# MoE steps ahead of the last score tile, shared squares, alternating PSUM banks and a reordered opening in a fused attention and mixture-of-depths kernel

## The chip, the cores and the metric

The kernel runs on one core of a Trainium2 chip. The metric is the device time of one execution in microseconds; the median of three runs of the kernel before is 230.48 us (229.37 to 230.82). The profiled execution took 229.61 us, with 227.8 us between its first and its last instruction; all times in a profile count from that first instruction.

Five engines work side by side, each through its own list of instructions in order: PE (TensorE) for matrix products and transposes, ACT (ScalarE), DVE (VectorE), Pool (GpSimd, here used nearly only to issue loads and stores) and SP (SyncE, which issues other transfers). An engine waits when its next instruction needs something that another engine or a transfer has not finished.

## The reference

Attention with squared ReLU in place of a softmax, for 8 batches of 12 heads, 448 tokens, 64 values a head; then a mixture-of-depths layer: of each batch's 448 tokens the 128 with the highest gate score go through a small two-layer network, and its gated result is added to their rows.

```python
scores = scale * np.matmul(q, k.transpose(0, 1, 3, 2))
attn = np.maximum(scores, 0.0) ** 2 / S
attn_out = np.matmul(attn, v)
x = attn_out.transpose(0, 2, 1, 3).reshape(B, S, H * D)      # (8, 448, 768)

scores = np.einsum('bsd,d->bs', x, w_gate)
out = x.copy()
for b in range(B):
    top_idx = np.argpartition(-scores[b], capacity)[:capacity]   # 128 of 448
    xe = x[b, top_idx]
    h = np.maximum(xe @ w1, 0.0)                                 # 768 -> 1024
    ye = h @ w2                                                  # 1024 -> 768
    g = 1.0 / (1.0 + np.exp(-scores[b, top_idx]))
    out[b, top_idx] = x[b, top_idx] + g[:, None] * ye
```

## The kernel before

Two heads make a pair, and a batch has six pairs (`hp` 0 to 5); there are 48 pairs (`t`). For a pair, PE transposes q and k into one PSUM bank, DVE copies them to SBUF, PE makes four score tiles (c = 0 to 3; the first three hold two heads side by side, the last one both heads' rest), ACT applies the ReLU on the way out of PSUM, DVE squares, and PE multiplies by v. The order of each engine's instructions is the order of the program's lines, so it can be read from the main loop.

PSUM has eight banks: score tiles take two buffers of two banks each, the transposes one, the attention output one, and the MoE steps two (`ma` and `mb`).

```python
    r_pool = ctx.enter_context(tc.tile_pool(name="r", bufs=6))
    a_pool = ctx.enter_context(tc.tile_pool(name="a", bufs=8))
    ...
    s_ps_pool = ctx.enter_context(tc.tile_pool(name="s_ps", bufs=2, space=PSUM))
    t_ps_pool = ctx.enter_context(tc.tile_pool(name="t_ps", bufs=1, space=PSUM))
    o_ps_pool = ctx.enter_context(tc.tile_pool(name="o_ps", bufs=1, space=PSUM))
    ma_ps_pool = ctx.enter_context(tc.tile_pool(name="ma_ps", bufs=1, space=PSUM))
    mb_ps_pool = ctx.enter_context(tc.tile_pool(name="mb_ps", bufs=1, space=PSUM))
    ...
    def begin():
        src = k[0, 0:2]
        nc.vector.memset(blank, 0.0)
        nc.scalar.activation(out=first, in_=blank[0:1, 0:1], func=AF.Sigmoid)
        busy(9, o_ps_pool, "o")                    # dummy matmuls on zeros
        nc.sync.dma_start(out=qf, in_=q[0, 0:2]...)         # plain fp32, pair 0
        nc.sync.dma_start(out=kf[:, 0, 0:4, :], ...)
        nc.sync.dma_start(out=kf[:, 1, 0:3, :], ...)
        nc.gpsimd.dma_start(out=k_sb[0][64:128, 0, 0:3, :], ...)   # casting loads
        nc.gpsimd.dma_start(out=k_sb[0][64:128, 1, 0:4, :], ...)
        ...
        load_q(0, 2, H)                            # heads 2 to 11 in one load
        load_kv(k_sb, k, 0, 2, H)                  # four loads
        load_kv(v_sb, v, 0, 0, H)
        ...                                        # three constants made on Pool
        load(1, 0, H)
        load(2, 0, H)
        nc.gpsimd.dma_start(out=w1_sb, ...)
        nc.gpsimd.dma_start(out=w2_sb, ...)
    ...
    def square(t, c):
        n = 2 if c < 3 else 1
        r = r_sb.pop((t, c))
        a = a_sb[t, c] = a_pool.tile([128, 2, S], BF16, name="a_sb")
        nc.vector.tensor_tensor(out=a[:, :n], in0=r[:, :n], in1=r[:, :n], op=ALU.mult)
    ...
    def evacuate(t):                               # attention output out of PSUM
        ...
        if hp in (0, 4, 5):
            nc.vector.tensor_scalar(out=xt, in0=o, scalar1=o_scale, ...)
        else:
            nc.scalar.activation(out=xt, in_=o, func=AF.Copy, scale=o_scale)
```

The MoE of a batch runs beside the attention of the next two: ranking and gathering of batch b - 1 and the network of batch b - 2. Tables say which step goes with which pair on which engine:

```python
    PE = {
        "rank": {0: [("gate", 0, 6)], 1: [("col",)], 5: [("xe", 0), ("sel",), ("xe", 1)]},
        "ffn": {0: [("h", 0)], 1: [("h", 1), ("h", 2), ("h", 3)],
                2: [("h", 4), ("h", 5), ("h", 6), ("h", 7)], 3: [("y", 0, 0, 8)],
                4: [("y", 1, 0, 8)]},
    }
    ACT = {
        "rank": {1: [("bc",)], 6: [("xeT", 1)]},
        "ffn": {2: [("hT", 0)], 3: [("hT", 1), ("sig",)], 4: [("gye", 0)], 5: [("gye", 1)]},
    }
    DVE = {
        "rank": {2: [("cols",), ("pieces",)], 3: [("rank", 1)], 4: [("rank", 3)],
                 6: [("chosen",), ("xeT", 0)]},
    }
    DVE2 = {
        "rank": {2: [("rank", 0)], 3: [("rank", 2)], 4: [("hot",)]},
    }
```

`h` is a block of the hidden layer (six matmuls; both halves of four blocks use `mb`), `hT` its ReLU, `y` a half of the second layer (`ma`, then `mb`), `gye` its gating, `xe` the gather of the chosen rows by a one-hot product. Entry 6 is done at the start of the next batch's pair 0. The main loop:

```python
        for t in range(NT):
            b, hp = divmod(t, NHP)
            scores(t, 0)
            scores(t, 1)
            relu(t, 0)
            relu(t, 1)
            moe(ACT, b, hp)
            if t == 0:
                busy(BUSY[0], mb_ps_pool, "m")     # 4 dummy matmuls
            if t > 0:
                square(t - 1, 3)
            moe(DVE, b, hp)
            if t + 1 < NT:
                transposes(t + 1)
            if t > 0:
                attend(t - 1)
                if hp not in (0, 1, 5):
                    evacuate(t - 1)
            if hp == 0 and 2 < b + 2 < B:
                load(b + 2, 0, H)
            scores(t, 2)
            relu(t, 2)
            square(t, 0)
            if t > 0 and hp in (0, 1, 5):
                evacuate(t - 1)
            square(t, 1)
            moe(DVE2, b, hp)
            scores(t, 3)
            relu(t, 3)
            square(t, 2)
            if b == 0:
                constants(hp)
                busy(BUSY[1], mb_ps_pool, "m")
            moe(PE, b, hp)
            ...                                    # late stores and scatters
        ...                                        # tail: the last two batches' MoE
```

Of the kernel before, what the change touches and what calls it, by code (L numbers as in the profile page):

```python
# [19 lines left out]
def kernel(  # L20
# [28 lines left out]
    r_pool = ctx.enter_context(tc.tile_pool(name="r", bufs=6))  # L49
    a_pool = ctx.enter_context(tc.tile_pool(name="a", bufs=8))  # L50
# [56 lines left out]
    kf = const.tile([64, 2, 4, Dh], FP32)  # L107
# [20 lines left out]
    def begin():  # L128

        src = k[0, 0:2]  # L130
# [3 lines left out]
        nc.sync.dma_start(out=qf, in_=q[0, 0:2].rearrange("h (p c) d -> p h c d", c=NC))  # L134
        nc.sync.dma_start(out=kf[:, 0, 0:4, :],
                          in_=src[0, 0:256].rearrange("(p c) d -> p c d", c=4))
        nc.sync.dma_start(out=kf[:, 1, 0:3, :],
                          in_=src[1, 0:192].rearrange("(p c) d -> p c d", c=3))
        nc.gpsimd.dma_start(out=k_sb[0][64:128, 0, 0:3, :],
                            in_=src[0, 256:S].rearrange("(p c) d -> p c d", c=3))  # L140
        nc.gpsimd.dma_start(out=k_sb[0][64:128, 1, 0:4, :],
                            in_=src[1, 192:S].rearrange("(p c) d -> p c d", c=4))
        nc.sync.dma_start(out=wg_cols, in_=moe_w_gate.rearrange("(m p) -> p m", p=128))
# [3 lines left out]
        nc.vector.memset(kf[:, 1, 3, :], 0.0)  # L147
        zero_halves(0)
        load_q(0, 2, H)
        load_kv(k_sb, k, 0, 2, H)  # L150
        load_kv(v_sb, v, 0, 0, H)
        nc.vector.tensor_copy(out=k_sb[0][0:64, 0:2], in_=kf)
# [69 lines left out]

    r_sb = {}

    def relu(t, c):
        n = 2 if c < 3 else 1
        r = r_sb[t, c] = r_pool.tile([128, 2, S], BF16, name="r_sb")
        nc.scalar.activation(out=r[:, :n], in_=s_ps.pop((t, c))[:, :n, :S], func=AF.Relu)  # L228

    def square(t, c):  # L230
        n = 2 if c < 3 else 1
        r = r_sb.pop((t, c))
        a = a_sb[t, c] = a_pool.tile([128, 2, S], BF16, name="a_sb")
        nc.vector.tensor_tensor(out=a[:, :n], in0=r[:, :n], in1=r[:, :n], op=ALU.mult)  # L234

    def attend(t):
# [3 lines left out]
        for c in range(4):  # L240
            a = a_sb.pop((t, c))
# [5 lines left out]

    def evacuate(t):
# [3 lines left out]
        if hp in (0, 4, 5):  # L252
# [18 lines left out]
    def moe_rank(b):  # L271
# [47 lines left out]
        def x_copy(c):  # L319
            nc.scalar.copy(out=xb[:P, c, :], in_=ps["x"])  # L320
# [193 lines left out]
    with tc.manual_schedule():  # L514
        begin()
        transposes(0)
        for t in range(NT):
# [8 lines left out]
            if t > 0:  # L526
                square(t - 1, 3)
# [102 lines left out]
```

## Time and profile before

| what | value |
|---|---|
| median of three runs | 230.48 us |
| span of the profiled execution | 227.8 us |
| PE, DVE, ACT, Pool busy | 202.2, 180.9, 182.0, 73.4 us |
| loads and stores moved | 39.89 MB, mean 175 GB/s |
| ReLU out of PSUM, 896 columns (x144) | 923 ns each |
| ReLU out of PSUM, 448 columns (x48) | 573 ns each |
| square, 896 and 448 columns (x144, x48) | 618 and 381 ns each |
| copy of the transposes (x48) | 654 ns each |
| evacuation on DVE, on ACT (x24 each) | 618 and 558 ns each |

A busy time is the time in which at least one instruction of the engine is under way. Instructions of one engine overlap at their ends: a matmul of 448 columns lasts 360 ns in the record, while the next one can follow 190 ns later, and a ReLU of 923 ns is followed by the next after some 820. So sums of durations overstate an engine's load, and the steps between starts say more. A row of the timeline gives start, length, engine, line, operation, output<-input, count, and in brackets how long the engine stood idle before it and what ended that.

### The profile page before, as it was taken

The numbers are of one execution on the slowest core, as the hardware profiler recorded it, in microseconds if no ns is written. First come the engines' busy times: TensorE is split into PE (matmuls) and PEld (weight loads), VectorE is DVE, ScalarE is ACT, GpSimd is POOL, SyncE is SP. The second block draws the span as 40 slices with busy tenths as digits, with TensorE's granted clock in tenths as the row PEclk, the third lists the DMA queues.
The fourth block names the chain that finished last, engine by engine and source line by source line (L and its number), as shares of the span: only waits on it lengthen the run. The fifth ranks groups of instructions, "written<-read, shape, count | busy, mean of one in ns | idle before, by whom it ended". The sixth has DMA issues, their size and how long they took to land.

```text
span 227.8 us, 5989 instructions
## 1 busy us (share of the span) xinstructions
PE 202.2 (89%) x2359; PEld 115.3 (51%) x2359; DVE 180.9 (79%) x437; ACT 182.0 (80%) x278; POOL 73.4 (32%) x101
## 2 busy tenths in 40 slices
PE   7379899968999999999999999999999999999920
PEld 3124344434666465646464556546654665457810
DVE  2158899998989898999799889889898989976310
ACT  3337998999889988998889979997999889964410
POOL 7793747210164352242315521320303210021220
PEclk9958999999999999999999999999999999999996
DMA  5999999999999999999999999999994957146643
GB/s 82 183 158 172 192 195 200 212 189 188 181 178 165 186 162 179 180 232 154 141 151 201 293 267 121 156 181 254 353 178 60 327 116 268 27 61 150 188 63 60
DMA packets 64220, 39.89 MB, mean 175 GB/s; under 512 B 37376, under 2 KB 61504, under 8 KB 63296
## 3 DMA queue, kind: packets, MB, share of 16 engines
q0 software_dynamic: 40160, 33.65, 94.1%
q1 hardware_dynamic: 24032, 5.86, 25.5%
q8 instruction: 18, 0.29, 0.6%
q14 instruction: 10, 0.08, 0.1%
HBM read 39.32 MB, written 14.16 MB: 235 GB/s over the span
## 4 chain that ended last, share of the span: by engine, by line
PE 47%; ACT 15%; DVE 15%; DMA 9%; issue 9%; POOL 2%; POOLq 1%; ACTq 0%; DVEq 0%
ACT r_sb L228 12%; PE s_ps L216 10%; PE o_ps L244 9%; DVE a_sb L234 8%; PE xe_ps L339 5%; PE ye_ps L406 4%; PE sc_ps L290 4%; PE t_ps L195 4%; PE h_ps L390 4%; DMA x_sb<-xT 3%; PE t_ps L201 3%; PE s_ps L220 3%; DMA k_sb<-in_k_dram 3%; DVE qkt L206 3%; DMA out_dram<-gye,idx 2%
## 5 line engine op out<-in xcount | busy, mean ns | idle before, releaser
L228 ACT ACTIVATE r_sb<-s_ps 128x896 bf16<-128x896 f32 x192 | 148.8, 835 | 23.9 <-PE s_ps L216 22.9
L234 DVE TENSOR_TENSOR a_sb<-r_sb 128x896 bf16<-128x896 bf16 x192 | 100.8, 559 | 6.9 <-ACT r_sb L228 5.9
L216 PE MATMUL s_ps<-qkt 64*128 64x448 bf16 x288 | 48.6, 360 | 6.5 <-ACT r_sb L228 4.1
L244 PE MATMUL o_ps<-a_sb,v_sb 128*64 128x448 bf16 x384 | 45.4, 356 | 0.4 <-DVE a_sb L234 0.4
L206 DVE COPY qkt<-t_ps 128x960 bf16<-128x960 bf16 x48 | 31.4, 654 | 17.5 <-PE t_ps L201 17.4
L216 PEld LDWEIGHTS <-qkt 64*128 64x128 bf16 x288 | 14.1, 93 | 40.0 <-issue 29.0
L444 POOL DMA_INDIRECT out_dram<-gye,idx x8 | 13.0, 1627 | 49.5 <-DVE a_sb L234 18.8
L94 POOL DMA_DIRECT2D v_sb<-in_v_dram x16 | 11.0, 685 | 43.6 <-DMA q_sb<-in_q_dram 18.8
L244 PEld LDWEIGHTS <-v_sb 128*64 128x64 bf16 x384 | 19.8, 111 | 8.6 <-issue 1.5
L390 PE MATMUL h_ps<-xeT,w_sb 128*128 128x128 bf16 x336 | 22.2, 219 | 0.8
L390 PEld LDWEIGHTS <-w_sb 128*128 128x128 bf16 x336 | 20.5, 97 | 4.0 <-issue 2.4
L201 PE MATMUL t_ps<-ident,k_sb 128*64 128x128 bf16 x384 | 19.7, 223 | 2.8 <-DMA k_sb<-in_k_dram 2.3
L323 DVE SCALAR_TENSOR_TENSOR trash<-bc,cols,tie 112x448 bf16<-112x448 f32 x32 | 21.7, 679 | 0.1
L195 PE MATMUL t_ps<-ident,q_sb 112*64 112x112 bf16 x384 | 18.9, 221 | 2.3 <-DMA q_sb<-in_q_dram 2.3
L406 PE MATMUL ye_ps<-w_sb,hT 128*128 128x384 bf16 x112 | 20.6, 326 | 0.0
L195 PEld LDWEIGHTS <-q_sb 112*64 112x64 bf16 x384 | 11.7, 111 | 16.0 <-issue 12.3
L220 PE MATMUL s_ps<-qkt 128*128 128x448 bf16 x48 | 17.3, 360 | 0.9 <-ACT r_sb L228 0.2
L91 POOL DMA_DIRECT2D v_sb<-in_v_dram x16 | 10.8, 677 | 20.9 <-PE s_ps L216 8.8
L201 PEld LDWEIGHTS <-k_sb 128*64 128x64 bf16 x384 | 13.7, 112 | 3.4 <-DMA k_sb<-in_k_dram 2.6
L253 DVE TENSOR_SCALAR xT<-o_ps 128x448 bf16<-128x448 f32 x24 | 14.8, 618 | 0.1
L406 PEld LDWEIGHTS <-hT 128*128 128x128 bf16 x112 | 10.8, 97 | 6.9 <-ACT hT L395 0.4
L255 ACT ACTIVATE xT<-o_ps 128x448 bf16<-128x448 f32 x24 | 13.4, 558 | 0.8 <-PE o_ps L244 0.8
(77 smaller groups left out, 185.1 us busy)
## 6 DMA issues: line engine op xcount, KB each, us to landing
out_dram<-x_sb POOLq DMA_DIRECT2D x8, 1344.0 KB, 15.1
q_sb<-in_q_dram POOLq DMA_DIRECT2D x7, 672.0 KB, 9.4
v_sb<-in_v_dram POOLq DMA_DIRECT2D x16, 192.0 KB, 12.6
w_sb<-in_moe_w_dram POOLq DMA_DIRECT2D x2, 1536.0 KB, 18.1
k_sb<-in_k_dram POOLq DMA_DIRECT2D x14, 192.0 KB, 14.4
v_sb<-in_v_dram POOLq DMA_DIRECT2D x16, 144.0 KB, 13.2
k_sb<-in_k_dram POOLq DMA_DIRECT2D x14, 144.0 KB, 14.5
x_sb<-xT SPq DMA_TRANSPOSE x42, 8.7
```

What stands on the lines that cost most here:

```text
L195: nc.tensor.matmul(out=ps[64 * hh:64 * hh + 64, c * P:(c + 1) * P], lhsT=qs[:, h0 + hh, c, :], rhs=ident[:P, :P], is_transpose=True, start ...
L201: nc.tensor.matmul(out=ps[64 * hh:64 * hh + 64, S + c * 128:S + (c + 1) * 128], lhsT=ks[:, h0 + hh, c, :], rhs=ident, is_transpose=True, s ...
L206: nc.vector.tensor_copy(out=sb, in_=ps)
L216: nc.tensor.matmul(out=ps[:, hh, :S], lhsT=sb[rows, S + c * 128:S + (c + 1) * 128], rhs=sb[rows, :S], start=True, stop=True)
L220: nc.tensor.matmul(out=ps[:, 0, :S], lhsT=sb[:, S + 384:S + 512], rhs=sb[:, :S], start=True, stop=True)
L228: nc.scalar.activation(out=r[:, :n], in_=s_ps.pop((t, c))[:, :n, :S], func=AF.Relu)
L234: nc.vector.tensor_tensor(out=a[:, :n], in0=r[:, :n], in1=r[:, :n], op=ALU.mult)
L244: nc.tensor.matmul(out=o_ps[t][rows, :], lhsT=vs[:, 2 * hp + hh, c, :], rhs=a[:, hh if c < 3 else 0, :], start=(c == 0), stop=(c == 3), sk ...
L253: nc.vector.tensor_scalar(out=xt, in0=o, scalar1=o_scale, scalar2=None, op0=ALU.mult)
L323: nc.vector.scalar_tensor_tensor(out=trash, in0=bc[:P, :], scalar=cols[:, c:c + 1], in1=tie[:, c, :], op0=ALU.subtract, op1=ALU.is_ge, acc ...
L390: nc.tensor.matmul(out=ps["h", f // 4][:, f % 4, :], lhsT=w1_sb[:, m, f * 128:(f + 1) * 128], rhs=xeT[:, m, :], start=(m == 0), stop=(m == ...
L406: nc.tensor.matmul(out=ps["y", half], lhsT=hT[:, f, :], rhs=w2_sb[:, f, cols_d], start=(f == 0), stop=(f == NF - 1))
```

## The change

It has four parts. The opening loads heads in the order in which pairs need them: pair 0's q, k and v come as plain fp32 through SP and ACT and are cast on chip, and Pool's casting loads go pair 1, then pairs 2 and 3, then v, then pairs 4 and 5. Tiles 1 and 2 of a pair share one buffer and one square. In batches 2 to 7, pairs 1 to 5, the first MoE step of a pair goes ahead of the last score tile on PE, so that PE has work while it waits for a score buffer. And the two MoE banks are taken in turn (`h` in `mb` then `ma`, `y` in `mb` then `ma`). With them some steps move: evacuations on DVE are those of pairs 0, 1 and 2, those on ACT of pairs 3, 4 and 5; `sig`, `pieces`, two rank steps and `hot` have other places, and in batch 1 one of four row copies goes to DVE.

```diff
-    r_pool = ctx.enter_context(tc.tile_pool(name="r", bufs=6))
-    a_pool = ctx.enter_context(tc.tile_pool(name="a", bufs=8))
+    r_pool = ctx.enter_context(tc.tile_pool(name="r", bufs=2))
+    a_pool = ctx.enter_context(tc.tile_pool(name="a", bufs=2))
 ...
     def begin():
+        def plain(dst, src, h, engine):
+            lo = 4 - h
+            for p0, n, rows in (0, lo, src[0, h, 0:64 * lo]), (64, 7 - lo, src[0, h, 64 * lo:S]):
+                engine.dma_start(out=dst[p0:p0 + 64, h, 0:n, :],
+                                 in_=rows.rearrange("(p c) d -> p c d", c=n))
+
+        nc.sync.dma_start(out=qf, in_=q[0, 0:2].rearrange("h (p c) d -> p h c d", c=NC))
+        plain(kf, k, 1, nc.scalar)
+        plain(kf, k, 0, nc.sync)
         nc.vector.memset(blank, 0.0)
         nc.scalar.activation(out=first, in_=blank[0:1, 0:1], func=AF.Sigmoid)
         busy(9, o_ps_pool, "o")
 ...
+        load_q(0, 2, 4)
 ...
-        load_q(0, 2, H)
-        load_kv(k_sb, k, 0, 2, H)
-        load_kv(v_sb, v, 0, 0, H)
-        nc.vector.tensor_copy(out=k_sb[0][0:64, 0:2], in_=kf)
+        load_kv(k_sb, k, 0, 2, 4)
+        plain(vf, v, 0, nc.sync)
+        plain(vf, v, 1, nc.sync)
+        nc.sync.dma_start(out=wg_cols, in_=moe_w_gate.rearrange("(m p) -> p m", p=128))
+        load_q(0, 4, 8)
+        load_kv(k_sb, k, 0, 4, 8)
+        load_kv(v_sb, v, 0, 2, H)
+        load_q(0, 8, H)
+        load_kv(k_sb, k, 0, 8, H)
 ...
+        nc.vector.tensor_copy(out=k_sb[0][:, 0:2], in_=kf)
 ...
+    GROUP = {0: (0, 0), 1: (1, 0), 2: (1, 1), 3: (2, 0)}
+    SHAPES = [1, 2, S], [2, 2, S], [1, 1, S]
 ...
-    def square(t, c):
-        n = 2 if c < 3 else 1
-        r = r_sb.pop((t, c))
-        a = a_sb[t, c] = a_pool.tile([128, 2, S], BF16, name="a_sb")
-        nc.vector.tensor_tensor(out=a[:, :n], in0=r[:, :n], in1=r[:, :n], op=ALU.mult)
+    def square(t, g):
+        r = r_sb.pop((t, g))
+        a = a_sb[t, g] = a_pool.tile([128, *SHAPES[g]], BF16, name=f"a_sb{g}")
+        nc.vector.tensor_tensor(out=a, in0=r, in1=r, op=ALU.mult)
 ...
+    VEC = 0, 1, 2
+    EARLY = 1, 2, 3, 4, 5
 ...
-        if hp in (0, 4, 5):
+        if hp in VEC:
             nc.vector.tensor_scalar(out=xt, in0=o, scalar1=o_scale, scalar2=None, op0=ALU.mult)
 ...
-        def hidden(f, pool=mb_ps_pool, tag="m"):
+        def hidden(f, pool=None, tag="m"):
             if f % 4 == 0:
+                pool = pool or (mb_ps_pool, ma_ps_pool)[f // 4]
 ...
-                pool = pool or (ma_ps_pool, mb_ps_pool)[half]
+                pool = pool or (mb_ps_pool, ma_ps_pool)[half]
                 ps["y", half] = pool.tile([CAP, 384], FP32, name="ye_ps", tag=tag)
 ...
     PE = {
-        "rank": {0: [("gate", 0, 6)], 1: [("col",)], 5: [("xe", 0), ("sel",), ("xe", 1)]},
+        "rank": {0: [("gate", 0, 6)], 1: [("col",)], 5: [("xe", 0, 1), ("xe", 1, 3), ("sel",), ("xe", 3, 6)]},
         "ffn": {0: [("h", 0)], 1: [("h", 1), ("h", 2), ("h", 3)],
-                2: [("h", 4), ("h", 5), ("h", 6), ("h", 7)], 3: [("y", 0, 0, 8)],
-                4: [("y", 1, 0, 8)]},
+                2: [("h", 4), ("h", 5), ("h", 6), ("h", 7)], 3: [("y", 0, 0, 2), ("y", 0, 2, 8)],
+                4: [("y", 1, 0, 2), ("y", 1, 2, 8)]},
     }
     ACT = {
         "rank": {1: [("bc",)], 6: [("xeT", 1)]},
-        "ffn": {2: [("hT", 0)], 3: [("hT", 1), ("sig",)], 4: [("gye", 0)], 5: [("gye", 1)]},
+        "ffn": {1: [("sig",)], 2: [("hT", 0)], 3: [("hT", 1)], 4: [("gye", 0)], 5: [("gye", 1)]},
     }
     DVE = {
-        "rank": {2: [("cols",), ("pieces",)], 3: [("rank", 1)], 4: [("rank", 3)],
+        "rank": {2: [("cols",)], 3: [("rank", 1)], 4: [("rank", 2)], 5: [("hot",), ("pieces",)],
                  6: [("chosen",), ("xeT", 0)]},
     DVE2 = {
-        "rank": {2: [("rank", 0)], 3: [("rank", 2)], 4: [("hot",)]},
+        "rank": {2: [("rank", 0)], 4: [("rank", 3)]},
 ...
             if t == 0:
+                nc.vector.tensor_copy(out=v_sb[0][:, 0:2], in_=vf)
                 busy(BUSY[0], mb_ps_pool, "m")
             if t > 0:
-                square(t - 1, 3)
+                square(t - 1, 2)
 ...
             square(t, 0)
-            if t > 0 and hp in (0, 1, 5):
+            if t > 0 and (t - 1) % NHP in VEC:
                 evacuate(t - 1)
+            moe(DVE2, b, hp)
             square(t, 1)
-            moe(DVE2, b, hp)
+            steps = moe_steps(b, hp)
+            if b > 1 and hp in EARLY and len(steps) > 1:
+                steps.pop(0)()
             scores(t, 3)
             relu(t, 3)
-            square(t, 2)
+            for step in steps:
+                step()
             if b == 0:
                 constants(hp)
                 busy(BUSY[1], mb_ps_pool, "m")
-            moe(PE, b, hp)
+            if b == 1 and hp in (2, 3, 4):
+                busy(hp, ma_ps_pool, "m")
```

The dummy matmuls in batch 1 (two, three and four of them) are new as well.

## The prediction

> **What bounds the kernel now.** I read the page first, then the busy time by batch, then the timeline of the opening and of one batch, and last the waits of the middle stretch.
>
> The page, with busy time, the granted clock and the DMA share in 40 slices of 5.7 us:
>
> ```profile
> PE 202.2 (89%) x2359; PEld 115.3 (51%) x2359; DVE 180.9 (79%) x437; ACT 182.0 (80%) x278; POOL 73.4 (32%) x101
> ...
> PEclk9958999999999999999999999999999999999996
> DMA  5999999999999999999999999999994957146643
> ```
>
> Three engines stand near 80% or above, so no single one is the bound; and the DMA row is full up to slice 30, so an earlier opening may run into the loads. The clock dips in slice 3. The same by stage (start of each batch's gate to the next):
>
> ```profile
> 0.00:14.00 14.00, 7.32 (x51) 3.01 (x51) 2.59 (x10) 3.83 (x5) 11.16 (x22) 0.92 1.07 144
> 14.00:37.70 23.70, 21.80 (x208) 10.02 (x207) 21.27 (x52) 20.05 (x28) 14.77 (x22) 0.90 1.41 180
> 37.70:61.80 24.10, 20.70 (x255) 11.52 (x254) 22.31 (x53) 22.91 (x34) 4.28 (x7) 1.00 1.24 194
> ...
> 85.70:109.70 24.00, 23.48 (x290) 13.59 (x288) 21.78 (x53) 22.02 (x35) 6.88 (x11) 1.00 1.63 181
> ```
>
> Columns: length, then busy us of PE, weight loads, DVE, ACT, Pool, then clock, DMA share, GB/s. A batch of six pairs takes 24.0 us; ACT works 22.0 of it. The first 14 us hold half their worth of work. Why, shows the timeline of the opening:
>
> ```profile
> 10.14 0.39 PE L195 MATMUL t_ps<-ident,q_sb 112*64 112x112 bf16 x8 [2.33 <-DMA q_sb<-in_q_dram]
> ...
> 13.10 0.61 PE L201 MATMUL t_ps<-ident,k_sb 128*64 128x128 bf16 x7 [1.19 <-DMA k_sb<-in_k_dram]
> 13.64 0.55 PE L216 MATMUL s_ps<-qkt 64*128 64x448 bf16 x2
> ```
>
> Pair 1's transposes wait for the one q load of ten heads (560 KB, 7.2 us from issue to landing) and for the four k loads behind it (about 7 us each), and the last two score tiles of pair 0 stand behind those transposes in PE's order: 6.39 to 13.64 us gives one pair's first half. In steady state, pair 1 of batch 3 (two PE lines and the ACT line of the next pair's first ReLU):
>
> ```profile
> 88.59 0.36 PE L216 MATMUL s_ps<-qkt 64*128 64x448 bf16 x2
> 88.99 0.35 PE L220 MATMUL s_ps<-qkt 128*128 128x448 bf16 x1
> 89.18 1.17 PE L390 MATMUL h_ps<-xeT,w_sb 128*128 128x128 bf16 x18
> ...
> 90.99 1.73 ACT L228 ACTIVATE r_sb<-s_ps 128x896 bf16<-128x896 f32 x2 [0.36 <-PE s_ps L216]
> ```
>
> A score tile takes 0.19 us of PE, so between 88.78 and 88.99 PE stands still: the last score tile needs the PSUM buffer that ReLU 1 still reads. Then come 1.4 us of MoE work, and the next pair's scores behind them; ACT idles 0.36 us for those. Over the whole middle (61.8 to 204.1 us):
>
> ```profile
> ACT r_sb L228 <- PE s_ps L216: 10.9, 23, 0.8
> ```
>
> That is the sum that better order in PE can win there: in a batch the idle pieces are 0.59, 0.36, 0.20 and 0.75 us, 1.9 of 24.0.
>
> **What the Trainium skill says.** "DMA: Bandwidth & Descriptors" ("Issuing engines are not separate DMA queues") says that loads started from SP, ACT and GpSimd share the same 16 engines; more issuers save issue time only. So what helps the opening is the order of bytes, not the extra queue. The trace agrees in kind: 224 KB of q from SP, ahead of everything, landed in 2.7 us, 560 KB behind other loads in 7.2. "TensorE: Matmul & The Clock Gate" ("Part 1: The HAM clock gate (the "warmup" mystery)") says an idle PE falls to half clock; the trace has 0.50 from 14 to 18 us, after PE's idle stretch from 7.8. "Perfetto Trace Analysis" ("Optimizing Tensor Performance", Matmuls) advises rotating independent groups through PSUM banks so that evacuation overlaps; here both halves of h use one bank, and at pair 2 the second half starts at 93.25, 0.3 us after the score tile (92.76 plus 0.19), just as ACT's 0.60 us copy from 92.60 ends. The same page ("Optimizing Scalar/DVE Operations") gives some 60 ns of fixed cost for a DVE operation on SBUF; three squares in a row took 1.69 us, one 0.618, so one step is 0.536 us, of which 0.474 is data (a square of 896 takes 618 ns, one of 448 takes 381, so 237 for each 448): 62 ns of fixed cost, in agreement.
>
> **Part by part.**
>
> *Opening.* Before, ten heads of q and k must land ahead of pair 1. After, Pool issues q of two heads first, then four small k loads: at 0.65 to 0.7 us an issue (rows of the trace), from 1.28 us, with the identity mask in between, the last leaves at about 5.2 us. By then 0.46 MB of plain q and k and 0.23 MB for pair 1 are asked for, 0.7 MB; before had moved 0.4 MB by 4 us and 1.06 MB by 9 us, so they land at about 7 to 8 us. The dummy matmuls of pair 0 end at 7.8 anyway. So the score tiles that came at 13.64 come at about 8.5: minus 5.1 us. PE no longer falls to half clock: pair 1 took 4.45 us (scores at 15.73, next at 20.18) against 3.9 for its successors, so minus 0.5. Against this: the loads of batch 0 are now 19 on Pool in place of 11, some 14 us of issue in a row, so batch 1's q goes out at about 17 us and not at 13.05. Its q and k (1.38 MB) at 190 GB/s are then down at about 26 us, just when transposes of pair 6 want them (t = 1 at about 10, then 3.7 us a pair). I put plus 0.8 for stalls there or at pairs 2 to 4. Sum: minus 4.8.
>
> *ACT against PE in batches 2 to 7.* ACT's work does not change: four ReLUs of a pair, start to start in a full queue, 3.02 us (97.69 to 100.70); copies add 0.42 (evacuation), 0.48 (hT), 0.46 (gye), 0.41 (bc), 0.36 (xeT), 0.09 (sigmoid). A batch is 6 x 3.02 + 3 x 0.42 + 2 x 0.48 + 2 x 0.46 + 0.86 = 22.1 us, the floor. The change moves evacuations from pairs 2, 3, 4 to pairs 4, 5, 0 of ACT's order, so need by pair goes from 3.38, 3.43, 3.92, 4.01, 3.90, 3.48 (pairs 0 to 5) to 3.80, 3.52, 3.50, 3.50, 3.90, 3.90. PE's own need is 1.78 to the third score tile, 0.38 for two tiles, and MoE steps of 1.47, 1.40, 1.35, 1.30, 1.30, 1.54: 3.63, 3.56, 3.51, 3.46, 3.46, 3.70. The early step (0.33 us of six h or two y matmuls, 0.22 of four gather ones) falls in the 0.2 us hole and the bank change takes away the 0.3 at pair 2. If only the larger need counts, the pairs take 3.80, 3.56, 3.51, 3.50, 3.90, 3.90 = 22.2. To that I add 0.3 for semaphores and 0.5 for DVE (below): 23.0, so minus 1.0 in each of six batches: minus 6.
>
> *DVE.* Shared squares: two of 618 ns give one of about 1.09 us (618 plus twice 237). In pitch that saves only 0.06 us a pair, 3 us of DVE over the run, beside other work. But the first of the two can no longer run while ReLU 2 runs: after ReLU 2 stand 1.0 us of shared square and 0.33 of the last. Attention of the pair wants it 1.26 us after ReLU 2 (94.42 to 95.68), so it just fits. At pair 2 DVE now carries squares, copy, an evacuation and a rank, about 3.8 us against 3.5 of ACT: 0.3 lost there, the larger part of my 0.5.
>
> *Batches 0 and 1.* In batch 1 ACT idles 1.2 of 24.1 and one 0.8 us row copy goes to DVE: minus 1.2. In batch 0 pairs 2 and 3 lost 0.4 us each before ACT's evacuation, which DVE now does: minus 0.7. *The tail* from 204 us keeps its order: 0.
>
> Sum: -4.8 - 6.0 - 1.2 - 0.7 = -12.7 from 230.5, about 217.8; I say 218.5, since small overlaps seldom all come off.
>
> **Rivals.** (a) *DMA becomes the bound of the early batches.* For: the share is full; batch 3's k takes 27 us to land and is down by about 67, its last v is issued at 62.9 and lands in 12.8, 75.7. With 11 us off, pair 18 would want k at about 71, v at 78. Against: slack of 2 to 4 us remains. If it binds, part of the opening's gain is given back: 222 to 225. (b) *The shared square turns into the wait:* attention waits for DVE in every pair, 0.3 us more; then batches stay at 23.7 and the opening alone counts: 223 to 225. For: the margin of 0.1 to 0.25 us. Against: ACT, not PE, is ahead of DVE by then. (c) *The early step delays the last score tile*, as 0.33 exceeds the hole of 0.2: but ReLU 2 covers 0.8 us, so nothing is lost. (d) *ACT runs dry nowhere*, 22.2 a batch: 213.
>
> **Range and chances.** The opening is nearly certain to give 3 to 6 us, and 2% is 4.6. The middle may give 2 to 9. So 213.5 to 224.5 should hold; chances 0.88 faster, 0.10 within 2%, 0.02 slower.
>
> **What would show it.** Right: pair 0's third score tile near 8.5 us, clock not below 0.9 in slice 3, a batch at 22.5 to 23.3, ACT's wait for scores in the middle down from 10.9 to under 5, a square of 1792 elements near 1.09 us. Wrong: PE waiting on k, q or v loads for more than 2 us in all after 9 us; attention waiting on the squares in each pair; a batch at 23.8 or more; a tail longer than 23.7.

## The result and the profile after

| | before | after |
|---|---|---|
| median | 230.65 us (229.37 to 231.4, four runs) | 222.01 us (221.65 to 222.49, four runs) |
| span of the profiled execution | 227.8 us | 220.2 us |

The ratio is 0.963, with a 95% interval of 0.959 to 0.968. The prediction was 218.5 us with a range of 213.5 to 224.5: the direction and the range hold, and the gain is 8.6 us where 12 were expected. The two profiled executions (229.61 and 221.93 us) are 7.7 us apart; the traces below account for these. The question is which terms of the sum fell short.

The page of the changed kernel, with the same lines as were shown of the kernel before:

```profile
PE 199.8 (91%) x2368; PEld 115.3 (52%) x2368; DVE 178.2 (81%) x394; ACT 181.3 (82%) x277; POOL 77.6 (35%) x109
...
PEclk9799999999999999999999999999999999999985
DMA  6999999999999999999999999999998999265543
```

DVE has 43 instructions fewer and 2.7 us less work, about the 3 us that the shared squares were to save. The low clock has moved from slice 3 to slice 2, so it is over by 11 us. Busy time by stage, cut at the first scores of pairs 1 and 6 and at the start of each batch's gate (columns: length, then busy us of PE, weight loads, DVE, ACT, Pool, then clock, DMA share, GB/s):

```profile
0.00:11.79 11.79, 8.76 (x56) 3.48 (x57) 4.41 (x16) 4.83 (x7) 10.57 (x21) 0.86 0.97 141
11.79:31.81 20.02, 16.84 (x172) 7.90 (x172) 17.58 (x40) 16.21 (x23) 15.66 (x25) 1.00 1.33 168
...
34.58:58.02 23.44, 21.90 (x264) 11.98 (x263) 21.42 (x47) 22.06 (x33) 7.30 (x10) 1.00 1.24 199
...
81.14:104.26 23.12, 22.94 (x292) 13.56 (x290) 21.23 (x46) 21.95 (x35) 10.98 (x16) 1.00 1.47 185
```

In a batch of the middle PE is now busy for all but 0.18 us, and ACT for all but 1.17. Where the time went, from the same starts in both traces:

| stretch | before, us | after, us | difference | predicted |
|---|---|---|---|---|
| start to pair 1's first scores | 15.73 | 11.79 | -3.94 | -5.1 (third tile) |
| pair 1 to pair 2 | 4.45 | 3.49 | -0.96 | -0.5 |
| pair 2 to pair 6 | 14.81 | 16.53 | +1.72 | +0.8 - 0.7 |
| pair 6 to the gate of batch 1 | 2.53 | 2.77 | +0.24 | 0 |
| batch 1 | 24.12 | 23.44 | -0.68 | -1.2 |
| batches 2, 3, 5, 6, each | 23.94, 23.93, 23.93, 23.93 | 23.12 | -0.8 | -1.0 |
| batch 4 | 24.56 | 23.20 | -1.36 | -1.0 |
| batch 7 | 22.10 | 22.04 | -0.06 | -1.0 |
| tail from the last gate | 23.78 | 24.42 | +0.64 | 0 |
| sum | 227.8 | 220.2 | -7.6 | -12.7 |

Three things are plain at once. Batch 7 never had a microsecond to give: it took 22.10 us before. Batch 4 of the kernel before was 0.6 us longer than its neighbours, for a reason that stays open, so 0.55 of its 1.36 us is luck. And batch 0, from pair 2 on, has become slower. The opening itself, on PE's timeline (start, length, operation, count, and in brackets the idle time ahead and what ended it):

```profile
6.05 0.41 PE L211 MATMUL t_ps<-ident,k_sb 128*64 128x128 bf16 x8 [1.11 <-DVE k_sb L162]
7.22 0.55 PE L226 MATMUL s_ps<-qkt 64*128 64x448 bf16 x4 [0.76 <-DVE qkt L216]
7.70 1.60 PE L127 MATMUL busy<-blank 128*128 128x448 bf16 x4
9.24 0.58 PE L205 MATMUL t_ps<-ident,q_sb 112*64 112x112 bf16 x8
...
10.18 0.56 PE L226 MATMUL s_ps<-qkt 64*128 64x448 bf16 x2
```

Pair 1's transposes follow the dummy matmuls with no wait for a load, which is what the new order of loads was for. But pair 0's k is there 0.8 us later than before (transposes at 6.05; they were at 5.22), and PE runs at half rate here: 1.60 us for four dummies which at full rate take 0.93. Third score tile: 10.18 where 8.5 was predicted. A steady pair, pair 1 of batch 3 (PE, then ACT):

```profile
84.26 0.36 PE L226 MATMUL s_ps<-qkt 64*128 64x448 bf16 x2
84.56 0.51 PE L412 MATMUL h_ps<-xeT,w_sb 128*128 128x128 bf16 x6
84.91 0.35 PE L230 MATMUL s_ps<-qkt 128*128 128x448 bf16 x1
85.09 0.83 PE L412 MATMUL h_ps<-xeT,w_sb 128*128 128x128 bf16 x12
```

```profile
86.57 1.73 ACT L243 ACTIVATE r_sb<-s_ps 128x896 bf16<-128x896 f32 x2 [0.31 <-PE s_ps L226]
```

The early block of h stands between the two score tiles as meant, and PE has no gap. ACT still idles 0.31 us for the next pair's scores. Over batches 2 to 7 (58 to 196 us) that wait sums to this:

```profile
ACT r_sb L243 <- PE s_ps L226: 6.8, 29, 0.3
```

It was 10.9 us, and under 5 was predicted.

### The profile page after: what moved, and what is told of

It reads as the page before. It is cut to its first block, busy times and chain, and to the rows that moved or that the text cites. A ratio compares the mean times of both kernels' runs of the same rounds, so it can differ in the third digit from the quotient of the medians.

```text
span 220.2 us, 5936 instructions
## 1 busy us (share of the span) xinstructions
PE 199.8 (91%) x2368; PEld 115.3 (52%) x2368; DVE 178.2 (81%) x394; ACT 181.3 (82%) x277; POOL 77.6 (35%) x109
## 4 chain that ended last, share of the span: by engine, by line
PE 55%; DVE 16%; ACT 15%; issue 6%; DMA 4%; POOLq 1%; SPq 0%; DVEq 0%; ACTq 0%
ACT r_sb L243 13%; PE s_ps L226 12%; PE o_ps L259 11%; DVE a_sb L248 10%; PE h_ps L412 9%; PE t_ps L205 4%; PE xe_ps L360 4%; PE sc_ps L310 4%; PE t_ps L211 3%; PE s_ps L230 3%; DMA out_dram<-gye,idx 3%; PE ye_ps L428 2%; DVE qkt L216 2%; DMA kf<-in_k_dram 2%; DVE trash L343 1%
## 5 line engine op out<-in xcount | busy, mean ns | idle before, releaser
L248 DVE TENSOR_TENSOR a_sb<-r_sb 128x896 bf16<-128x896 bf16 x144 | 96.6, 696 | 15.1 <-ACT r_sb L243 13.8
L259 PE MATMUL o_ps<-a_sb,v_sb 128*64 128x448 bf16 x384 | 45.9, 353 | 2.7 <-DVE a_sb L248 2.6
L226 PEld LDWEIGHTS <-qkt 64*128 64x128 bf16 x288 | 15.0, 93 | 38.5 <-issue 26.4
L259 PEld LDWEIGHTS <-v_sb 128*64 128x64 bf16 x384 | 19.8, 110 | 12.2 <-issue 4.8
L94 POOL DMA_DIRECT2D v_sb<-in_v_dram x16 | 10.9, 679 | 41.9 <-DMA q_sb<-in_q_dram 11.8
L412 PE MATMUL h_ps<-xeT,w_sb 128*128 128x128 bf16 x336 | 24.4, 219 | 0.0
L428 PE MATMUL ye_ps<-w_sb,hT 128*128 128x384 bf16 x112 | 22.8, 327 | 0.0
L211 PE MATMUL t_ps<-ident,k_sb 128*64 128x128 bf16 x384 | 19.1, 221 | 1.1 <-DVE k_sb L162 1.1
L94 POOL DMA_DIRECT2D k_sb<-in_k_dram x20 | 13.3, 665 | 5.7 <-DMA k_sb<-in_k_dram 2.3
L273 DVE TENSOR_SCALAR xT<-o_ps 128x448 bf16<-128x448 f32 x24 | 14.8, 617 | 0.0
L91 POOL DMA_DIRECT2D k_sb<-in_k_dram x20 | 13.5, 673 | 3.4 <-PE xe_ps L360 1.3
```

What stands on the lines that cost most here:

```text
L91: nc.gpsimd.dma_start(out=t[0:64, hs, 0:lo, :], in_=src[b, hs, 0:64 * lo].rearrange("h (p c) d -> p h c d", c=lo))
L94: nc.gpsimd.dma_start(out=t[64:128, hs, 0:hi, :], in_=src[b, hs, 64 * lo:S].rearrange("h (p c) d -> p h c d", c=hi))
L211: nc.tensor.matmul(out=ps[64 * hh:64 * hh + 64, S + c * 128:S + (c + 1) * 128], lhsT=ks[:, h0 + hh, c, :], rhs=ident, is_transpose=True, s ...
L226: nc.tensor.matmul(out=ps[:, hh, :S], lhsT=sb[rows, S + c * 128:S + (c + 1) * 128], rhs=sb[rows, :S], start=True, stop=True)
L248: nc.vector.tensor_tensor(out=a, in0=r, in1=r, op=ALU.mult)
L259: nc.tensor.matmul(out=o_ps[t][rows, :], lhsT=vs[:, 2 * hp + hh, c, :], rhs=a[:, hh if c < 3 else 0, :], start=(c == 0), stop=(c == 3), sk ...
```

## The experiments

All kernels are compared with runs of the kernel before on the same chip. Medians are of all executions; ratios leave out those that took over 1.5% longer than the fastest of their kernel. A batch length is that on which most of the batches 2 to 6 of a profile agree; single batches, the fourth or the sixth above all, were up to 1.2 us longer, and those that were longer still are told. "places" means the pair and engine at which evacuations, `sig`, `pieces`, rank steps and `hot` stand.

**1. Without the early step.**

```diff
-    EARLY = 1, 2, 3, 4, 5
+    EARLY = ()
```

> The changed kernel without the early MoE step (all PE steps of a pair after its last score tile again; everything else as changed). Theory (the hole ahead of the last score tile was about 0.1 us a pair, not 0.2, so the early step is a small part; banks and places of steps give the rest): 1 to 3 us slower than the changed kernel's 222.0, a batch at 23.3 to 23.6 in place of 23.12. Rival (the early step is what shortened the batches from 23.94 to 23.12): 4 to 6 us slower, a batch back near 23.9.

Measured: 223.54 us, ratio 0.973 (0.962 to 0.984); batches of 23.27 us. The early step is worth 0.15 us a batch, no more. The reason is on PE's timeline of this kernel, pairs 1 and 2 of batch 3:

```profile
84.63 0.36 PE L226 MATMUL s_ps<-qkt 64*128 64x448 bf16 x2
84.92 0.36 PE L230 MATMUL s_ps<-qkt 128*128 128x448 bf16 x1
...
88.31 0.36 PE L226 MATMUL s_ps<-qkt 64*128 64x448 bf16 x2
88.71 0.35 PE L230 MATMUL s_ps<-qkt 128*128 128x448 bf16 x1
```

From the third score tile to the fourth is 0.29 us in pair 1, with nothing put between, and with the early step 0.30 passes to the block of h. So those 0.3 us are no wait for a buffer. The third tile's two matmuls have 64 rows each; where another such pair follows, it starts 0.19 us later (four matmuls last 0.55 us, two 0.36), but in these traces a matmul of all 128 rows never follows in less than 0.29 us, be it a score tile, a block of h or a part of y. Only what is above it, 0.1 us in pair 2, is a hole.

**2. The MoE banks as before.** `h` in `mb` alone, `y` in `ma` and then `mb`; the early step stays.

```diff
-                pool = pool or (mb_ps_pool, ma_ps_pool)[f // 4]
+                pool = pool or mb_ps_pool
...
-                pool = pool or (mb_ps_pool, ma_ps_pool)[half]
+                pool = pool or (ma_ps_pool, mb_ps_pool)[half]
```

> The changed kernel with the MoE banks as before (both halves of h in one bank, the halves of y in the other order), early step kept. Theory (the bank order is what lets the early step and the gather run without waiting for ACT's copies): 3 to 5 us slower than 222.0; PE waits for hT at pair 2 (0.5 us) and for gye at pair 5 (0.3 us), a batch at 23.6 to 23.9. Rival (banks matter little, those waits lie beside ACT's work): within 1 us of 222.0.

Measured: 227.14 us, ratio 0.989 (0.978 to 1.001); batches of 23.99 us, slightly beyond the theory's 23.9 and longer than before the whole change. PE and ACT at pair 2 of batch 3:

```profile
87.50 0.36 PE L226 MATMUL s_ps<-qkt 64*128 64x448 bf16 x2
88.39 0.49 PE L412 MATMUL h_ps<-xeT,w_sb 128*128 128x128 bf16 x6 [0.52 <-ACT hT L417]
88.72 0.35 PE L230 MATMUL s_ps<-qkt 128*128 128x448 bf16 x1
```

```profile
87.74 0.60 ACT L417 ACTIVATE hT<-h_ps 128x512 bf16<-128x512 f32 x1
...
90.42 1.73 ACT L243 ACTIVATE r_sb<-s_ps 128x896 bf16<-128x896 f32 x2 [0.76 <-PE s_ps L226]
```

The early block of h wants the bank that ACT is copying out, waits 0.52 us for it, and now the score tile waits behind it. ACT pays with 0.76 us in place of 0.25.

**3. Both: banks as before and no early step** (the edits of 1 and 2 together; one run).

> The changed kernel with the MoE banks of before and no early step; places of the other steps, shared squares and opening as changed. Theory (the early step is a loss where it has to wait for the bank, since the wait then stands ahead of the last score tile): a batch at 23.5 to 23.8, shorter than the 23.99 with old banks and the early step. Rival (the early step is a gain of 0.15 us whatever the banks): a batch at 24.1 to 24.2.

Measured: 225.75 us; batches of 23.69. With the old banks the early step costs 0.30 us a batch; with the new ones it gains 0.15. So the parts don't add up one by one, and in order the middle of the change reads: 23.93 before, 23.69 with the new places, 23.27 with the banks in turn as well, 23.12 with the early step.

**4. The kernel before with the banks in turn alone** (the edit of 2, the other way round, in the kernel before).

> The kernel before with the MoE banks in turn alone (h in mb then ma, y in mb then ma). Theory (the waits of PE for hT at pair 2 and gye at pair 5 are 0.3 and 0.2 us; undoing the banks in the changed kernel cost 0.87 us a batch because the early step stood in front of the wait): a batch at 23.4 to 23.7 in place of 23.94, time 227 to 229. Rival (banks alone carry the whole 0.8 us): a batch at 23.1 to 23.2, time 224 to 225.

Measured: 227.51 us, ratio 0.994 (0.990 to 0.998); batches of 23.59. Alone the banks give 0.34 us a batch, as predicted for pair 2 (0.3).

**5. The changed kernel with the steps and evacuations in their old places.**

```diff
-    VEC = 0, 1, 2
+    VEC = 0, 4, 5
...
-        "ffn": {1: [("sig",)], 2: [("hT", 0)], 3: [("hT", 1)], ...
+        "ffn": {2: [("hT", 0)], 3: [("hT", 1), ("sig",)], ...
...
-        "rank": {2: [("cols",)], 3: [("rank", 1)], 4: [("rank", 2)], 5: [("hot",), ("pieces",)],
+        "rank": {2: [("cols",), ("pieces",)], 3: [("rank", 1)], 4: [("rank", 3)],
...
-        "rank": {2: [("rank", 0)], 4: [("rank", 3)]},
+        "rank": {2: [("rank", 0)], 3: [("rank", 2)], 4: [("hot",)]},
```

> The changed kernel with evacuations, sig, pieces, ranks and hot in the places that they had before; early step, banks, shared squares and opening as changed. Theory (ACT's load per pair was uneven, 3.4 to 4.0 us, and evening it out let PE and ACT run in step): a batch at 23.4 to 23.7, 2 to 4 us slower than 222.0. Rival (only PE's order counts now, PE being busy 22.94 of 23.12): a batch at 23.1 to 23.2, no slower.

Measured: 226.57 us, ratio 0.983 (0.977 to 0.990); batches of 23.51 (two of the profile were 24.43 and 24.11). The places are worth 0.39 us a batch on top of the rest. Batch 1 takes 24.13 us here, as before the change (24.12), so its gain hangs on the places too. In batch 0 they change next to nothing: pair 2 to pair 6 takes 16.44 us here, 16.53 in the changed kernel. DVE has no evacuation in pairs 2 and 3 of this kernel, and waits instead for the ReLU of tile 2, without which the shared square cannot start:

```profile
20.65 1.09 DVE L248 TENSOR_TENSOR a_sb<-r_sb 128x1792 bf16<-128x1792 bf16 x1 [0.76 <-ACT r_sb L243]
```

**6. Four squares a pair in place of the shared one.**

```diff
-    GROUP = {0: (0, 0), 1: (1, 0), 2: (1, 1), 3: (2, 0)}
-    SHAPES = [1, 2, S], [2, 2, S], [1, 1, S]
+    GROUP = {0: (0, 0), 1: (1, 0), 2: (2, 0), 3: (3, 0)}
+    SHAPES = [1, 2, S], [1, 2, S], [1, 2, S], [1, 1, S]
...
-            moe(DVE2, b, hp)
             square(t, 1)
+            moe(DVE2, b, hp)
+            square(t, 2)
```

> The changed kernel with four squares a pair again, in the order of before (tile 1's square ahead of ReLU 2's end, own buffers), everything else as changed. Theory (the shared square made attention of batch 0 wait for DVE, 0.3 to 0.6 us a pair): 1 to 2 us faster than 222.0, from the start of pair 1's scores to pair 6's 18 to 18.8 us in place of 20.02, batches 2 to 6 unchanged at 23.1. Rival (sharing saves DVE 62 ns a pair and with that the batches): 0.5 to 3 us slower, batches at 23.3 or more.

Measured: 222.49 us in the middle of four runs that spread from 219.49 to 229.39, too wide for a ratio. The trace is clearer than the times: batches 2 and 3 take 23.12 us as with the shared square (4 to 6 took 23.23 to 23.48 in this execution, but 23.12 to 23.43 with the same squares in experiment 9), so sharing gains and costs nothing there that these runs resolve. But pair 2 to pair 6 of batch 0 takes 15.53 us, not 16.53. DVE of the changed kernel over one pair of batch 0:

```profile
17.73 0.64 DVE L216 COPY qkt<-t_ps 128x960 bf16<-128x960 bf16 x1
18.29 0.61 DVE L248 TENSOR_TENSOR a_sb<-r_sb 128x896 bf16<-128x896 bf16 x1
18.82 0.61 DVE L273 TENSOR_SCALAR xT<-o_ps 128x448 bf16<-128x448 f32 x1
19.52 1.09 DVE L248 TENSOR_TENSOR a_sb<-r_sb 128x1792 bf16<-128x1792 bf16 x1
20.71 0.22 DVE L78 MEMSET k_sb<- 64x192 uint32 x1
...
21.75 0.32 DVE L248 TENSOR_TENSOR a_sb<-r_sb 128x448 bf16<-128x448 bf16 x1
21.99 0.64 DVE L216 COPY qkt<-t_ps 128x960 bf16<-128x960 bf16 x1
```

and what PE does meanwhile:

```profile
17.86 0.38 PE L259 MATMUL o_ps<-a_sb,v_sb 128*64 128x448 bf16 x2 [0.66 <-DVE a_sb L248]
...
22.12 0.38 PE L259 MATMUL o_ps<-a_sb,v_sb 128*64 128x448 bf16 x2 [0.67 <-DVE a_sb L248]
```

In pairs 2 and 3 DVE works without a gap, for 4.26 and 4.04 us: in batch 0 it also fills constants (in pair 2 four memsets, 1.2 us), and it, not ACT or PE, is the bound there. In pairs 4 and 5 it has no evacuation, and idles ahead of the shared square as in experiment 5, where in experiment 6 it squares tile 1 meanwhile and waits 0.22 and 0.41 us:

```profile
27.96 1.09 DVE L248 TENSOR_TENSOR a_sb<-r_sb 128x1792 bf16<-128x1792 bf16 x1 [0.76 <-ACT r_sb L243]
```

Three times the attention waits for the last square. On the page, all such waits of the run come to 2.6 us, and the timeline has them in batch 0 (0.66, 0.67, 0.44) and at the very last pair (0.79), nowhere between:

```profile
L259 PE MATMUL o_ps<-a_sb,v_sb 128*64 128x448 bf16 x384 | 45.9, 353 | 2.7 <-DVE a_sb L248 2.6
```

**7. The kernel before with the new opening alone** (`begin` and the fp32 tiles of the change, its casts, nothing else).

> The kernel before with the new opening alone (loads in the order of use, pair 0's v cast on chip). Theory (the opening's whole gain of 3.9 us at pair 1's scores is kept, since the old squares of batch 0 do not wait): 226 to 227.5, pair 6's scores near 31 us in place of 34.99. Rival (DMA takes the gain back at batch 1 or 3, where loads land just in time): 228.5 to 230, with PE waiting for q, k or v loads after 20 us.

Measured: 227.22 us, ratio 0.987 (0.977 to 0.997). Pair 6's first scores come at 30.42 us, against 34.99 before and 31.81 in the changed kernel; pair 2 to pair 6 takes 15.13 us. So the opening by itself brings 4.6 us to the start of pair 6, close to the 4.8 that I gave it; the rest of the change takes 1.4 of them back in batch 0. Its time is 2.4 us below the 229.58 us of the kernel before on its chip, less than that; one late batch of its profile, which is of the slowest execution (228.78 us), took 27.42 us (see the last section).

**8. Without pair 0's four dummy matmuls.**

```diff
-    BUSY = 4, 3
+    BUSY = 0, 3
```

> The changed kernel without the four dummy matmuls of pair 0. Theory (pair 1's transposes start at 9.24 us because those matmuls, at half clock, end then, and not because of a load): transposes of pair 1 at 7.7 to 8.0 us, pair 1's scores 1 to 1.6 us earlier than 11.79, time 220.5 to 221.5. Rival (pair 1's loads land only at about 9 us): transposes wait for a load, scores of pair 1 stay at 11.5 to 12, time unchanged.

Measured: 222.21 us, ratio 0.968 (0.963 to 0.973), so no gain over the changed kernel that these runs resolve. In the trace pair 1's transposes start at 7.57 us, with no wait for a load, and pair 1's scores at 10.85. The loads would allow another 1.7 us; the dummies, not the loads, hold the third tile. What was gained in the opening (0.9 to 1.1 us at pairs 1 and 6) is not seen in the time. One batch of the profile took 27.49 us, but the profile is of an execution of 225.18 us; why the four near 222 us were no faster stays open.

**9. Experiments 6 and 8 together.**

> The changed kernel with four squares a pair again and without pair 0's dummy matmuls. Theory (the two gains add): pair 1's scores near 10.4 us, pair 6's near 29.5 in place of 31.81, time 219 to 220.5. Rival (what the opening gains waits for loads at batch 1 or 3): PE waits for q, k or v after 20 us, time 221 or more.

Measured: 222.09 us, ratio 0.970 (0.962 to 0.977); pair 6 at 31.67 us and not near 29.5, batches of 23.12. PE ran at half rate from 9.7 to about 16 us here, and pair 1 to pair 2 took 5.07 us where the changed kernel took 3.49; that took the opening's gain. No load stalled PE after 20 us, so the rival's cause is not seen either.

**10. Four squares, more warm-up ahead of the first scores, none behind them:** twelve dummies at the start, three between pair 0's transposes and its scores.

```diff
-    BUSY = 4, 3
+    BUSY = 0, 3
...
-        busy(9, o_ps_pool, "o")
+        busy(12, o_ps_pool, "o")
...
         transposes(0)
+        busy(3, o_ps_pool, "o")
```

> The changed kernel with four squares a pair, and with the dummy matmuls of the opening moved: 12 in place of 9 at the start, 3 between pair 0's transposes and its scores, none after its scores. Theory (PE's clock falls to half in the opening because PE stands idle from 5 to 7.2 us, and half clock costs the first two pairs 1 to 2 us): clock at 1.0 by 8 us, pair 1's scores at 9.5 to 10.3, pair 6's at 28.8 to 29.8, time 1.5 to 3 us below the changed kernel. Rival (the clock follows its own course, or ACT and DVE bind the first pairs): pair 1's scores at 11 to 12, time as the changed kernel.

Measured: 227.24 us, six runs from 218.81 to 237.47. The opening of the profile came as hoped: full rate from 6.5 us, pair 1 at 10.36, pair 6 at 29.72, the gate of batch 1 at 32.25 in place of 34.58, then batches of 23.12 to 125 us. That the moved dummies did it is not shown: with the dummies where they were, PE of experiment 2 ran at full rate from 6 us too, and pair 1 came at 10.43. Then two batches took 29.16 and 33.32. ACT of this kernel:

```profile
142.12 0.58 ACT L433 ACTIVATE gye<-ye_ps,g 128x384 f32<-128x384 f32 x1 [2.51 <-DMA out_dram<-gye,idx]
...
176.79 0.58 ACT L433 ACTIVATE gye<-ye_ps,g 128x384 f32<-128x384 f32 x1 [8.06 <-DMA out_dram<-gye,idx]
```

The gated result of batch b goes into one of three buffers, and the scatter-add that empties the buffer of batch b - 3 had not landed. This is no proof of a better kernel.

**11. The changed kernel once more**, in five rounds.

> The changed kernel itself once more, on the same chip as the one beside it, to compare with: 221.5 to 222.5 us, batches at 23.12.

Measured: 223.14 us, ratio 0.969 (0.962 to 0.976); six runs from 221.73 to 226.56. The batches are 23.12 us again; the opening is not the same: half rate until 12.9 us, pair 1 at 12.89, pair 6 at 32.36.

**12. Half of the network's products left out:** in batches 0 to 6, three of the six products of each block of `h` and four of the eight of each half of `y` are not computed.

```diff
-            for m in range(NM):
+            for m in (0, 1, NM - 1):
...
-            for f in range(f0, f1):
+            for f in (f for f in range(f0, f1) if f < 2 or f > 5):
```

> The changed kernel with part of the network left out in batches 0 to 6: three of the six products of each hidden block, and four of the eight of each half of the second layer, are not computed, so about 1.5 us and 1.3 us less of PE work a batch (0.065 us a product of 128 columns, 0.16 us one of 384), in pairs 0 to 4; nothing is taken from ACT or DVE. The changed kernel's batches take 23.12 us, of which ACT works 21.95. Theory: the 1.15 us in which ACT still idles are waits for the next pair's first score tile, because the PE work of each pair (PE busy 22.94 of 23.12) exceeds what ReLU needs; then batches come down to 21.9 to 22.3 us, the idle pieces of ACT in pairs 1 to 4 go below 0.1 us each, and the whole run to about 216 to 218. Rival: the rest above ACT's work is semaphores and DVE's extra work of pair 2, as the prediction's sum of 0.3 and 0.5 us had it; then batches stay at 22.8 to 23.1 and the run within 2 us of the changed kernel's.

Measured: 221.88 us, between two runs near 217 and two near 227 (216.98, 217.40, 226.37, 227.31); ratio 0.946 (0.938 to 0.954). The batches of the profile up to 125 us take 22.26 to 22.27 us, inside the theory's 21.9 to 22.3 and far from the rival's 22.8. ACT in batch 3:

```profile
83.59 0.53 ACT L314 COPY bc<-sc_ps 128x448 f32<-128x448 f32 x1
84.00 3.12 ACT L243 ACTIVATE r_sb<-s_ps 128x896 bf16<-128x896 f32 x4
87.01 0.60 ACT L417 ACTIVATE hT<-h_ps 128x512 bf16<-128x512 f32 x1
87.48 3.12 ACT L243 ACTIVATE r_sb<-s_ps 128x896 bf16<-128x896 f32 x4
```

Four ReLUs without a break; no wait for scores above 0.04 us is left in pairs 1 to 5, and 0.20 in pair 0. From one pair's first scores to the next, pairs 0 to 5 take 3.84, 3.52, 3.47, 3.48, 3.89, 4.07 us; in the changed kernel 3.95, 3.80, 3.71, 3.69, 3.90, 4.07. So PE's products bound pairs 1, 2 and 3 of the changed kernel and a little of pair 0, while pairs 4 and 5 don't change with them and are ACT's. (This is the profile of the 226.37 us run; its late batches show the wait of experiment 10 again, 5.6 us at once.)

## Why the prediction was right, and where it was not

**Opening, -5.1 for the third score tile, -0.5 for the clock, +0.8 for loads.** What the loads were to do is right: no wait of PE for q, k or v after 9 us, and alone the opening is worth 4.6 us at pair 6. That this is so near 4.8 is luck, since the three terms missed apart: in experiment 7 the third tile came 3.3 us earlier, pair 1 to pair 2 took 1.3 us less, and pair 2 to pair 6 0.3 us more.

The first term was too large. I had "the dummy matmuls of pair 0 end at 7.8 anyway" from the old timeline. They end at 9.24, since pair 0's k comes 0.8 us later and the dummies run at half rate. Where PE happened to run at full rate (experiment 2), the tile came at 9.06:

```profile
7.17 0.55 PE L226 MATMUL s_ps<-qkt 64*128 64x448 bf16 x4 [0.76 <-DVE qkt L216]
7.65 0.93 PE L127 MATMUL busy<-blank 128*128 128x448 bf16 x4
8.51 0.39 PE L205 MATMUL t_ps<-ident,q_sb 112*64 112x112 bf16 x8
...
9.06 0.36 PE L226 MATMUL s_ps<-qkt 64*128 64x448 bf16 x2
```

So about 1.1 of the 1.7 us is the rate, the rest fits the later k. The last of k's plain loads is issued as before (1.83 us, 1.82 before) but lands at 5.44 and not at 4.62; what slows it, among the loads now asked for around it, was not taken apart. The kernels with the new opening all have pair 0's scores at 7.1 to 7.6 us, those with the old one at 6.4 to 6.5.

The second term failed as a mechanism: PE did fall to half rate, from 7.7 to 11 us in the changed kernel and until 12.9 in experiment 11. The half rate moved, it didn't go. And 0.8 us of the same stretch come and go with the old opening: pair 1 to pair 2 took 4.44 us in the profile before and 3.64 in that of experiment 4, so most of the measured -0.96 can't be laid to the loads. The 0.8 for stalls on loads at pairs 2 to 6 did not come: PE waited there for squares, not for loads.

**Batch 0, evacuation to DVE, -0.7.** This step failed, with the wrong sign. I counted the 0.4 us for which ACT waited ahead of an evacuation as time to win, and did not ask what DVE, which also fills constants in this batch, would do. From pair 2 to pair 6 the kernel before takes 14.8 us, with the new opening 15.1 (experiment 7), with the places as changed but four squares 15.5 (experiment 6), and with the shared square 16.5.

The first step, 0.3, is within the spread of the three profiles with the steps of before (14.8 to 15.1). The second, 0.4, is the evacuations: experiments 6 and 7 differ in batch 0 only in them and in numbers of buffers, and in the two pairs with an evacuation more on DVE its copies follow each other after 4.15 and 3.75 us in place of 3.93 and 3.52. The third and largest is the shared square: 16.3 to 16.65 us in eight profiles with it, 15.3 to 16.0 in three without it and with the same places, so 0.8 to 1.0. It can start only when the ReLU of tile 2 is done, where the first of two squares ran during that ReLU. Put into that wait, an evacuation costs nothing (experiment 5), so the two steps do not simply add.

**Batches 2 to 7, -1.0 each.** The size is nearly right (23.12 for 23.0), by partly wrong reasons. The floor of ACT, 22.1, is right: 21.95 of work, and 22.27 us when PE is made light, with pairs within 0.04 us of the need that I gave ACT in all but pair 5. The 0.3 "for semaphores" is not borne out: 0.24 of the 0.32 us between 21.95 and 22.27 are waits for score tiles in pairs 0 and 1. The 0.5 "for DVE" is wrong: 0.85 us go away with PE's products, so they are PE's. My needs of PE for pairs 1 to 3 (3.56, 3.51, 3.46) were too small by 0.24, 0.20 and 0.23; 0.11 of each is the step from the third tile to a matmul of all rows, 0.30 us and not the 0.19 that I took for every tile. The step back costs about as much: in pair 3 of batch 3 of the changed kernel, six y products that follow each other every 0.16 us start at 92.50, and the next pair's scores at 93.57, 0.1 us later than a seventh product would. By the same error "the 0.2 us hole" of a pair was 0.1 or nothing, and the early step, which was to fill it, gave 0.15 us a batch in all. The banks gave their 0.3 alone, 0.42 after the places, and 0.87 with the early step. And batch 7 was counted in the six although it took 22.10 us before: that is a plain slip, worth 0.9 us.

**Batch 1, -1.2,** came as -0.7. With the old places it is not there at all (24.13 us in experiment 5, where the row copy stays on DVE), so the row copy that I named does not bring it alone.

**Shared square, 1.09 us.** Measured 1.09. It fits in the middle: no attention of batches 1 to 6 waits for DVE. My own figures did not say so: 1.0 and 0.33 us after ReLU 2 are more than the 1.26 us that I set against them.

**The tail, 0,** became +0.64. The order on the engines is indeed kept: from the last gate to DVE's last gating is 14.03 us in both traces. The two last scatters differ; before, and then after:

```profile
213.48 1.56 POOL L444 DMA_INDIRECT out_dram<-gye,idx  x1 [4.11 <-ACT gye L411]
...
219.68 1.56 POOL L444 DMA_INDIRECT out_dram<-gye,idx  x1 [4.64 <-DMA out_dram<-gye,idx]
```

```profile
205.37 1.56 POOL L466 DMA_INDIRECT out_dram<-gye,idx  x1 [4.47 <-ACT gye L433]
...
211.84 1.56 POOL L466 DMA_INDIRECT out_dram<-gye,idx  x1 [4.90 <-DMA out_dram<-gye,idx]
```

The last one waits for the one ahead to land, 6.47 us after that one's start and not 6.20, and its own way to the end is 8.31 and not 8.12 us. With the 0.2 us by which the first starts later, that is the 0.64. It can't be laid to the change: experiment 7, which has the tail of before, took 24.39 us for it, and the changed kernel itself 24.19 when it ran once more.

**The rivals.** (a), DMA as the bound of the early batches, did not come as told: no load stalls PE. But transfers showed as a limit in another place (last section). (b), the shared square as the wait of every pair, is wrong for the middle; in batch 0 the shared square does cost time. (c) holds only with the banks in turn; with the old ones the early step delays the last tile of pair 2 by 0.8 us (1.22 us behind the third tile in experiment 2, 0.40 in experiment 3). (d), 22.2 a batch, is what half of the network's products would give.

**The signs.** Of those named for right, the batch length (23.12), the clock of slice 3 and the square came; the third tile (10.18 us) and ACT's wait for scores (6.8) did not. Of those for wrong only the tail came, and its limit of 23.7 lay below what the kernel before already took.

Of the 5.1 us between the sum of -12.7 and the measured -7.6, batch 0 with its opening makes 2.6, batches 2 to 7 make 1.3, the tail 0.6 and batch 1 0.5.

## What to carry to other kernels

Before counting an engine's need by "tiles times pitch", read the pitch of each shape behind which another shape follows: one row-split tile ahead of a full matmul, 0.11 us longer than assumed, was half of the hole that the early step was to fill, and that step gave 0.15 us a batch. Work put ahead of a wait must not carry a wait of its own: the same early step costs 0.3 us where its bank is still being read and gains 0.15 where it isn't, so such parts have to be tried together. And when work is moved to the engine that looks free on average, or merged on it, check the stage in which that engine has other things to do, here the first batch with its constants: a merged operation starts only when its last input is there.

## What the runs showed of the hardware

The half rate of the first matmuls ends at different times in different executions of the same instructions: pair 1's scores came at 10.43 to 12.94 us in eight profiles that share the opening up to there. "TensorE: Matmul & The Clock Gate" (Part 1, "What's actually happening") of the Trainium skill says that the activity window runs freely, so that the number of slow matmuls varies from run to run; the traces agree that it varies, and don't show the window itself. But the granted clock of the profile reads 1.00 in stretches in which matmuls take twice their time, as here in the repeat of the changed kernel, where the four dummies at 8.31 us took 1.68 us for 0.93 (the 1.00 behind the five engines' busy times is the clock):

```profile
8.00:10.00 2.00, 2.00 (x9) 0.52 (x8) 0.55 (x1) 1.73 (x2) 1.93 (x3) 1.00 1.53 158
```

In the changed kernel's first profile the column does read 0.50 from 8 to 10 us. So in the opening the length of a known matmul tells the rate more surely than that column.

The second thing is a limit close behind the changed kernel. In three profiles, those of experiments 7, 10 and 12, ACT stood 2 to 8 us for a scatter-add to land, and the batch with it; in the chain of waits of experiment 10 (start, length, what) a q load and then the scatter are the path:

```profile
123.83 31.27 DMA q_sb<-in_q_dram
...
156.99 19.78 DMA out_dram<-gye,idx
```

The changed kernel's scatter of 146.80 us is followed by the ACT step that needs its buffer at 165.03 and landed in 10.5 to 12.2 us in this stretch, so it has some 6 to 8 us to spare. "Perfetto Trace Analysis" ("DMA Instruction — SWDGE (GPSIMD)") says that such a row on Pool ends when the descriptors are written, not when the data are moved; the trace agrees, with a row of 1.6 to 2.4 us for landings of up to 21.5. A kernel with a faster opening reaches that ACT step earlier, which fits, but all three profiles were of longer executions than the fastest of their kernel, and why a load takes 31 us then stays open; more buffers for the gated result were not tried. Open too is a stand of PE of 2.97 us in experiment 8, ahead of a matmul for which the profile shows no wait:

```profile
117.04 0.10 PEld L428 LDWEIGHTS <-hT 128*128 128x128 bf16 x1 [2.97 <-issue]
```

A transfer of the queue that the profile calls instruction, q8, took 2.5 us there, from 113.2 us on, where most of its 18 take about 1; whether PE waited for it is not shown.
